# Sigmoid attention and a clipped MLP in one kernel: a third batch multiplied in native float32 beside the first MoE product, with ScalarE's order written out

## The chip, the cores and the metric

The kernel runs on one core of one Trainium2 chip. The metric is the device time of one execution in microseconds. A core has a matrix engine (TensorE, PE), a vector engine (VectorE, DVE), an activation engine (ScalarE, ACT), a general engine (GpSimd, POOL) and a queue that only issues transfers (SyncE, SP). Each takes its instructions in the order in which they stand; they wait for each other through semaphores.

## What is computed

Eight batches of twelve heads, 448 tokens, head size 64. Attention uses a sigmoid in place of a softmax, and its output goes through an MLP with a clipped gate (called MoE here). All inputs are float32 except that the two weight matrices come as float64 (the reference's weights are never cast down).

```
scores = scale * np.matmul(q, k.transpose(0, 1, 3, 2)) - np.log(S)
attn = 1.0 / (1.0 + np.exp(-scores))
x = np.matmul(attn, v)          # then (B, H, S, D) -> (B*S, H*D) = 3584 x 768
h = x @ w_in                    # 768 x 2048
g = h * np.clip(h + 3.0, 0.0, 6.0) / 6.0
out = g @ w_out                 # 2048 x 768
```

## The kernel before

**Units.** Two heads form a pair `p`; a batch has 6 pairs, so there are 48. A pair has `NST` = 4 steps: three over 128 keys of both heads, one over the last 64 keys. Step `s` is step `s % 4` of pair `s // 4`; `scores(s)` issues the products of k and q and the sigmoid of their sum, `av(s)` the products of v and the sigmoid. The tokens of all batches are also cut into seven blocks of 512; `moe_in(t)` yields the 288 products of block `t` with w_in, 18 for each of 16 columns `fc`, evacuates each column's PSUM tile `ph` (two buffers) through ACT and DVE into `g`, and stores `g` in DRAM (`gd`). A last stage multiplies `g` by w_out; the change doesn't touch it.

**Two kinds of product.** In the first `NB` = 2 batches (pairs below `PA` = 12) PE multiplies float32 as it is ("native"): one product for each head, on half of PE's rows or columns, two heads side by side; the profile counts two instructions for each. From the third batch on, every operand is split into a high and a low part (`qh`, `ql`, `ka`, `ah`, `al`), and three or four faster products take the place of one. The split costs work elsewhere: `prep` and `prep_block` cast and subtract on DVE, POOL and ACT, each sigmoid is computed twice (`ah`, `a`, L209 and L210), and DVE subtracts them (`al`, L211).

**w_in.** It comes as float64 and is decoded in 32 chunks of 128x384 by `split_f64`: a transfer, then on ACT an absolute value (L51, "Abs" below), five DVE steps (L52 to L58), a sum on POOL (L61), a cast on ACT (L62) that is the high part, and a subtraction on POOL (L63) that is the low part. Column `fc` needs chunks 2`fc` and 2`fc`+1. A chunk stands in borrowed buffers: the pair `qh`/`ql`, or `pend`.

**Order.** PE's order is the order of the code. All other engines are ordered by a scheduler with a timeline of its own. The code runs the 48 native steps in rounds of two (`scores(s)`, `scores(s+1)`, `av(s-2)`, `av(s-1)`), and asks for 24 chunks in them; then it issues 72 products of block 0 (`EX`) with the other 8 chunks; then the third batch's 24 split steps, with 216 products of block 0 spread among them, nine a step. In fact the scheduler has all 32 chunks decoded by the end of the native steps. From step 72 on, each batch's 24 steps carry the 288 products of one block. At step 73 `flush` turns the columns of the last batch that belong to the next block (`pend`) into high and low parts: six casts and six subtractions.

Of the kernel before, what the change touches and what calls it, by code (L numbers as in the profile page):

```python
# [9 lines left out]
F32 = mybir.dt.float32  # L10
# [8 lines left out]
P = 128  # L19
# [19 lines left out]
NWE = 8
NEA = 5  # L40
# [3 lines left out]
halves = (slice(0, D), slice(D, P))  # L44


def split_f64(nc, hi, lo, st, a, b):

    low, high = st[:, :, 0], st[:, :, 1]
    ai, bi = a.bitcast(I32), b.bitcast(I32)  # L50
    nc.scalar.activation(a, high.bitcast(F32), AF.Abs, bias=0.0, scale=2.0**-112)  # L51
    nc.vector.tensor_scalar_min(a, a, F64_TOP)  # L52
    nc.vector.tensor_scalar(out=ai, in0=ai, scalar1=3, scalar2=None, op0=ALU.logical_shift_left)
    nc.vector.scalar_tensor_tensor(  # L54
        out=ai, in0=high, scalar=-(2**31), in1=ai, op0=ALU.bitwise_and, op1=ALU.bitwise_or
    )
    nc.vector.tensor_scalar(out=bi, in0=ai, scalar1=-(2**23), scalar2=None, op0=ALU.bitwise_and)  # L57
    nc.vector.scalar_tensor_tensor(  # L58
        out=b, in0=low.bitcast(U32), scalar=2.0**-52, in1=b, op0=ALU.mult, op1=ALU.mult
    )  # L60
    nc.gpsimd.tensor_tensor(out=a, in0=a, in1=b, op=ALU.add)  # L61
    nc.scalar.copy(hi, a)  # L62
    nc.gpsimd.tensor_tensor(out=lo, in0=a, in1=hi.bitcast(F32), op=ALU.subtract)  # L63
# [13 lines left out]
def tile_kernel(ctx: ExitStack, tc: tile.TileContext, qk, vP, wi, wo, outT):  # L77
# [39 lines left out]
    def load_native(p):  # L117
        b, hp = divmod(p, NP)
        t = att.tile([P, 2, S], F32, tag="ka", name=f"qkn_{p}")
        v = att.tile([P, 2 * NC, D], F32, tag=("vv", "vv", "vr")[p % 3], name=f"vn_{p}", bufs=(2, 2, 1)[p % 3])  # L120
        nc.sync.dma_start(out=t, in_=qk[b, hp])
        for j in range(2):
            nc.sync.dma_start(out=kbn[p % 3][halves[j], halves[j]], in_=qk[b, hp, halves[j], 1, NC * P :])
        nc.sync.dma_start(out=v, in_=vP[b, hp, :, : 2 * NC])
        for j in range(2):
            nc.sync.dma_start(out=vbn[p % 3][halves[j], halves[j]], in_=vP[b, hp, halves[j], 2 * NC])
        ops[p] = t[:, 0], t[:, 1], v
# [88 lines left out]
    def block(t, cc):  # L216
# [3 lines left out]
            xb[t, cc] = x[:, 0], x[:, 1]  # L220
        return xb[t, cc]

    def flush(b):

        t, c0, _, n = pieces(b)[1]
        for cc in range(NCC):
            xh, xl = (x[:, c0 : c0 + n] for x in block(t, cc))
            x = pend[b][:, cc, :n]
            nc.vector.tensor_copy(xh, x)
            nc.vector.tensor_tensor(out=xl, in0=x, in1=xh.bitcast(F32), op=ALU.subtract)  # L230

    def av(s):
        p, c = divmod(s, NST)
        b, hp = divmod(p, NP)
        last = c == NC
        if p < PA:
            if c == 0:
                pv[p] = ps_a.tile([P, 512], F32, tag=f"pv{p % 2}", name=f"pv_{p}")
            _, a = at.pop(s)
            pt, v = pv[p], ops[p][2]  # L240
            for j in range(2):
                v_, a_ = (vbn[p % 3][:, halves[j]], a[:, 0]) if last else (v[:, j * NC + c], a[:, j])
                nc.tensor.matmul(pt[halves[j], :S], v_, a_, start=(c == 0), stop=last)
            if last:
                for t, c0, q0, n in pieces(b):
                    xh, xl = (x[:, c0 : c0 + n] for x in block(t, hp))
                    nc.scalar.copy(xh, pt[:, q0 : q0 + n])
                    nc.vector.tensor_tensor(out=xl, in0=pt[:, q0 : q0 + n], in1=xh.bitcast(F32), op=ALU.subtract)
            return
        vv = ops[p][3]  # L250
        if c == 0:
            pv[p] = [ps_a.tile([P, 512], F32, tag=f"pv{u}", name=f"pv{u}_{p}") for u in range(2)]
        sc, ah, al = at.pop(s)
        if last:
            vbh, vbl = blk[p % 2]["vbh"], blk[p % 2]["vbl"]
# [8 lines left out]
            nc.gpsimd.tensor_tensor(out=xl, in0=x[:, :n], in1=xh.bitcast(F32), op=ALU.subtract)
            for _, _, q0, n in rest:
                if b not in pend:
                    pend[b] = xpl.tile([P, NCC, PEND], F32, tag="pend", name=f"pend_{b}")
                nc.vector.tensor_tensor(out=pend[b][:, hp, :n], in0=out[:, q0 : q0 + n], in1=x[:, q0 : q0 + n], op=ALU.add)
            return
        for a_ in (ah, al):  # L270
            for j in range(2):
                nc.tensor.matmul(  # L272
                    pv[p][j][:, :S], vv[:, j, c, :], a_[:, j],
                    start=(c == 0 and a_ is ah), stop=(c == NC - 1 and a_ is al),
                )
        if c == NC - 1:
# [8 lines left out]
    evac = []  # L285

    def load_wi(n):
        fc, u = divmod(n, 2)
        hc = NCC // 2
        w = hc * P  # L290
        if u == 0:
            wt = win[fc // GF].tile([P, 2, NCC, P], F32R, tag=f"wi{fc}", name=f"wi_{fc}")
            wih[fc], wil[fc] = wt[:, 0], wt[:, 1]
        cs = slice(u * hc, (u + 1) * hc)
        hi, lo = (w_[fc][:, cs].rearrange("p c f -> p (c f)") for w_ in (wih, wil))
        if n % 3 == 2:
# [27 lines left out]
    nwi = 0
    load_native(0)
    load_native(1)
    for s in range(0, SB, 2):
        p, c = divmod(s, NST)
        scores(s)
        scores(s + 1)  # L330
        for u in (s - 2, s - 1):
            if u >= 0:
                av(u)
        if c == 2 and p + 2 < PA:
            load_native(p + 2)
        if p == PA - 2 and c == 0:
            load(PA)
        while nwi < NWA and nwi * SB < (s + 2) * NWA:
            load_wi(nwi)
            nwi += 1  # L340
        if s == 0:
            for u in range(2):
                for t in blk[u].values():
                    for j in range(2):
                        nc.gpsimd.tensor_copy(t[halves[j], halves[1 - j]], vbn[0][halves[j], halves[1 - j]])
    av(SB - 2)
    av(SB - 1)

    moe = moe_in(0)
    for n in range(EX):  # L350
        while nwi < 2 * NFC and (nwi - NWA) * NBW <= n:
            load_wi(nwi)
            nwi += 1
        next(moe)
# [5 lines left out]
    for s in range(SB, NSTEP + 1):  # L360
        p, c = divmod(s, NST)
        b = p // NP
        if s < NSTEP:
# [4 lines left out]
                prep(p + 1)  # L368
            if c == 3 and p + 2 < B * NP:
                load(p + 2)  # L370
        if s % BS == 1 and s > SB + BS:
            for _ in moe:
                pass
            flush(b - 1)
            moe = moe_in(b - 2)
        if s > SB:
            quota += KM if s > SB + BS else KM - EX / BS
        for _ in range(KB if c == 0 else KM):
            if quota >= 1:
                next(moe, None)  # L380
# [16 lines left out]
    def load_wo(ec, pool):  # L397
# [4 lines left out]
        for u in range(NFC * P // WPC):  # L402
# [105 lines left out]
```

## Time and profile before

| | |
|---|---|
| median of 3 runs | 1306.04 us (1305.58 to 1306.68) |
| profiled execution | 1307.34 us, of which the span is 1305.5 |
| PE busy in the span | 1251.2 us (96%) |
| DVE busy | 814.4 us (62%) |
| ACT busy | 556.9 us (43%) |
| POOL busy | 370.2 us (28%) |
| transfers | 145.87 MB, mean 112 GB/s |
| native stage | 0 to 143 us |

The share of busy time is a mean over stages with different limits; a stage has to be read by itself, by who waits there for whom. A row of the timeline gives the start and the length in us, the engine, the line, what is written from what, and in brackets the idle time before it and what ended it. In a row by groups the columns behind the bar are busy us in all, mean ns of one, and idle time before with its releasers. A row of the waits gives us in total, how often, and the longest.

### The profile page before, as it was taken

The page shows a single profiled execution, that of the slowest core. Times are in us where ns is not written, and L with a number is a line of the kernel's source. Part 1 is how long each engine was busy: PE and PEld are TensorE (multiplying, and loading weights), DVE is VectorE, ACT ScalarE, POOL GpSimd, SP SyncE. Part 2 cuts the span into 40 slices and gives each one's busy share as a digit, 9 for nine tenths or more (in the row PEclk, how much of TensorE's full clock was granted, in tenths as well). Part 3 has the DMA queues.
Part 4 walks back from the last instruction along what each step waited for, and adds up shares of the span by engine and source line. Part 5 has one row for each costly group of instructions (what it writes and reads, how often), then busy time and mean ns, then how long its engine had stood idle before and what let it go on. Part 6 is the DMA issues. An engine that isn't in the chain of part 4 may idle for free.

```text
span 1305.5 us, 15392 instructions
## 1 busy us (share of the span) xinstructions
PE 1251.2 (96%) x5496; PEld 990.4 (76%) x5496; DVE 814.4 (62%) x1362; ACT 556.9 (43%) x716; POOL 370.2 (28%) x392
## 2 busy tenths in 40 slices
PE   6776999999999999999999999999999999999998
PEld 1222588788888888888888887787888888888887
DVE  5977589988988888888898658968130303030300
ACT  4565367665666656665666644424020202020200
POOL 4565334333333333333333224554000000000000
PEclk9789999999999999999999999999999999999999
DMA  7554433343334333334333137743322222222000
GB/s 212 166 154 137 120 106 103 103 119 103 111 105 119 106 100 100 112 111 111 111 112 104 48 114 242 265 146 128 113 85 93 85 92 86 92 85 93 25 25 25
DMA packets 67566, 145.87 MB, mean 112 GB/s; under 512 B 10912, under 2 KB 35488, under 8 KB 63904
## 3 DMA queue, kind: packets, MB, share of 16 engines
q1 hardware_dynamic: 67488, 144.87, 35.5%
q8 instruction: 44, 0.72, 0.2%
q14 instruction: 34, 0.28, 0.1%
HBM read 104.46 MB, written 40.37 MB: 111 GB/s over the span
## 4 chain that ended last, share of the span: by engine, by line
PE 74%; DVE 13%; DMA 5%; issue 3%; ACT 2%; POOL 2%; SPq 1%; POOLq 0%; ACTq 0%; DVEq 0%
PE po L461 30%; PE ph L312 28%; PE pv L272 6%; PE sc L204 3%; PE sc L205 3%; DMA ws<-wo 2%; PE sc L258 2%; DMA wis<-wi 1%; PE sc L201 1%; DVE wa L54 1%; DMA wiqh<-wi 1%; DVE wb L58 1%; DVE wb L57 1%; DVE ql L152 1%; DVE g L317 1%
## 5 line engine op out<-in xcount | busy, mean ns | idle before, releaser
L312 PE MATMUL ph<-x,wi 128*128 128x512 f32 x2016 | 497.9, 394 | 4.8 <-DVE g L317 3.8
L312 PEld LDWEIGHTS ph<-x,wi 128*128 128x128 f32 x2016 | 377.9, 188 | 86.3 <-DVE g L317 6.3
L461 PE MATMUL po<-gh,wol 128*128 128x512 f32 x672 | 262.4, 390 | 1.0 <-POOL wol L63 1.0
L461 PE MATMUL po<-gh,woh 128*128 128x512 f32 x672 | 262.2, 390 | 1.2 <-ACT woh L62 1.2
L461 PE MATMUL po<-gl,woh 128*128 128x512 f32 x672 | 262.0, 390 | 0.0
L468 DVE TENSOR_SCALAR o<-po 128x512 f32<-128x512 f32 x42 | 29.0, 690 | 292.7 <-PE po L461 292.7
L211 DVE TENSOR_TENSOR al<-a,ah 128x896 fp32r<-128x896 f32 (+1 forms) x144 | 170.0, 1181 | 56.7 <-ACT a L210 55.7
L421 ACT CAST gh<-gr 128x2048 fp32r<-128x2048 f32 x28 | 53.4, 1912 | 288.3 <-PE po L461 288.2
L209 ACT ACTIVATE ah<-sc,bias_s 128x896 fp32r<-128x896 f32 (+1 forms) x144 | 131.8, 915 | 80.2 <-PE sc L201 38.7
L148 POOL TENSOR_TENSOR ka<-qkr,ka 64x448 fp32r<-64x448 f32 x72 | 111.7, 1552 | 146.7 <-issue 126.7
L461 PEld LDWEIGHTS po<-gh,wol 128*128 128x128 f32 x672 | 126.5, 188 | 28.1 <-POOL wol L63 1.8
L461 PEld LDWEIGHTS po<-gh,woh 128*128 128x128 f32 x672 | 126.6, 188 | 27.9 <-ACT woh L62 1.6
L461 PEld LDWEIGHTS po<-gl,woh 128*128 128x128 f32 x672 | 126.6, 188 | 26.2
L210 ACT ACTIVATE a<-sc,bias_s 128x896 f32<-128x896 f32 (+1 forms) x144 | 131.1, 911 | 9.5 <-DVE al L211 8.5
L316 ACT ACTIVATE g<-ph,bias 128x512 f32<-128x512 f32 x112 | 77.2, 689 | 63.6 <-PE ph L312 58.8
L158 POOL TENSOR_TENSOR vv<-vr,vv 128x192 fp32r<-128x192 f32 x72 | 42.6, 611 | 171.9 <-issue 168.1
L317 DVE SCALAR_TENSOR_TENSOR g<-g,ph 128x512 f32<-128x512 f32 x112 | 76.2, 680 | 16.7 <-ACT g L316 16.2
L422 DVE TENSOR_TENSOR gl<-gr,gh 128x2048 fp32r<-128x2048 f32 x28 | 63.9, 2288 | 27.4 <-ACT gh L421 27.4
L204 PE MATMUL sc<-qh,ka 128*128 128x448 f32 x216 | 79.2, 367 | 0.1
L205 PE MATMUL sc<-ql,ka 128*128 128x448 f32 x216 | 79.1, 366 | 0.0
L152 DVE TENSOR_TENSOR ql<-qkr,qh 128x896 fp32r<-128x896 f32 x36 | 68.9, 1913 | 4.7 <-ACT qh L151 0.9
L192 PE MATMUL sc<-qkn 64*128 64x448 f32 x144 | 41.6, 681 | 25.2 <-ACT a L194 21.1
(84 smaller groups left out, 1354.6 us busy)
## 6 DMA issues: line engine op xcount, KB each, us to landing
qkr<-qk SPq DMA_DIRECT2D x144, 224.0 KB, 4.1
gd<-g SPq DMA_DIRECT2D x112, 256.0 KB, 2.6
gr<-gd SPq DMA_DIRECT2D x28, 1024.0 KB, 5.6
ws<-wo SPq DMA_DIRECT2D x24, 512.0 KB, 4.5
outT<-o SPq DMA_DIRECT2D x42, 256.0 KB, 2.0
wiqh<-wi SPq DMA_DIRECT2D x22, 384.0 KB, 3.4
vr<-vP SPq DMA_DIRECT2D x36, 224.0 KB, 2.5
qkn<-qk SPq DMA_DIRECT2D x12, 448.0 KB, 4.1
```

The lines of the kernel that those rows point to most:

```text
L148: nc.gpsimd.tensor_tensor(out=ka[other, j], in0=kr[other, j], in1=ka.bitcast(F32)[other, j], op=ALU.subtract)
L152: nc.vector.tensor_tensor(out=ql, in0=qr, in1=qh.bitcast(F32), op=ALU.subtract)
L204: nc.tensor.matmul(sc[:, j, :S], ka[:, j, cs], qh[:, j], start=True, stop=False)
L205: nc.tensor.matmul(sc[:, j, :S], ka[:, j, cs], ql[:, j], start=False, stop=True)
L209: nc.scalar.activation(ah[:, js], sc[:, js, :S], AF.Sigmoid, bias=bias_s, scale=scale)
L210: nc.scalar.activation(a[:, js], sc[:, js, :S], AF.Sigmoid, bias=bias_s, scale=scale)
L211: nc.vector.tensor_tensor(out=al[:, js], in0=a[:, js], in1=ah.bitcast(F32)[:, js], op=ALU.subtract)
L272: nc.tensor.matmul(pv[p][j][:, :S], vv[:, j, c, :], a_[:, j], start=(c == 0 and a_ is ah), stop=(c == NC - 1 and a_ is al),)
L312: nc.tensor.matmul(ph, w[:, cc], x, start=(n == 0), stop=(n == 3 * NCC - 1))
L316: i1 = nc.scalar.activation(g, ph, AF.Relu, bias=bias_3, scale=1.0)
L317: i2 = nc.vector.scalar_tensor_tensor(out=g, in0=g, scalar=6.0, in1=ph, op0=ALU.min, op1=ALU.mult)
L461: nc.tensor.matmul(po[t, ec], w[:, fc], x[:, u], start=(fc == 0 and n == 0), stop=(fc == NFC - 1 and n == 2))
```

## The change

`NB` = 3: the third batch is native too, so there are 72 native steps and 18 native pairs. The first 48 run as before, with 17 chunks (`NWA`) asked for instead of 24. In the other 24, twelve rounds, each round has 23 products of block 0 (`K2`) behind its two native steps: 276 of the 288. The other 12 come behind step 72's scores; the 72 products in a block of their own are gone. The remaining 15 chunks are asked for in these rounds, 1.5 a round.

`split_f64` is cut in two. `load_wi` is a generator with stages: the transfer; then, two rounds later (one round later from chunk 17 on), `join_f64` with Abs, the DVE steps and POOL's sum; then, one round later, `split_f32` with ACT's cast and POOL's subtraction. `feed` takes every chunk on its way one stage further in each round. A fourth place to stand in is added: chunks may also use the buffer `qkr`, the raw q and k of a split pair. The third of the native v tiles goes to the buffer of `qp0` instead of `vr`, so that pair 18's v can be loaded early. A native batch's columns for the block after next go into `pend` by a copy and are split by `flush`.

ACT's order, like PE's, is the order of the code in all 72 native steps. Outside them, and on DVE, POOL and SP, the scheduler decides as before.

```diff
-PA = 2 * NP
+NB = 3
+PA = NB * NP
+P0 = (NB - 1) * NP
-EX = 72
-NWA = 24
-NBW = 9
+K2 = 23
+NWA = 17
+NWG = 1.5
+NSL = 4
...
-def split_f64(nc, hi, lo, st, a, b):
+def join_f64(nc, st, a, b):
...
     nc.gpsimd.tensor_tensor(out=a, in0=a, in1=b, op=ALU.add)
+
+def split_f32(nc, hi, lo, a):
     nc.scalar.copy(hi, a)
     nc.gpsimd.tensor_tensor(out=lo, in0=a, in1=hi.bitcast(F32), op=ALU.subtract)
...
-                for t, c0, q0, n in pieces(b):
+                for u, (t, c0, q0, n) in enumerate(pieces(b)):
+                    if u and b == NB - 1:
+                        hold(b)
+                        nc.vector.tensor_copy(pend[b][:, hp, :n], pt[:, q0 : q0 + n])
+                        continue
...
-        if n % 3 == 2:
+        own = n % NSL if n < NWA else n % (NSL - 1)
+        if own == 2:
+            sa = att.tile([P, 4 * w], I32, tag="qkr", name=f"wis_{n}", bufs=1)
+            st, ab = sa[:, : 2 * w], sa[:, 2 * w :]
+        elif own == 3:
...
         nc.sync.dma_start(out=st, in_=wi[fc, :, u * w : (u + 1) * w])
-        split_f64(nc, hi, lo, st, ab[:, :w], ab[:, w:])
+        yield
+        if n < NWA:
+            yield
+        join_f64(nc, st, ab[:, :w], ab[:, w:])
+        yield
+        split_f32(nc, hi, lo, ab[:, :w])
...
+    with tc.manual_schedule(engines={mybir.EngineType.PE, mybir.EngineType.Activation}):
+        load_native(0)
+        feed(1)
+        load_native(1)
+        for s in range(0, SB, 2):
...
+            if s < P0 * NST:
+                feed((s + 2) * NWA // (P0 * NST) + 1)
+            else:
+                feed(NWA + int((s + 2 - P0 * NST) / 2 * NWG) + 1)
+                if p == PA - 2 and c == 2:
+                    load(PA)
+                moe = moe or moe_in(0)
+                for _ in range(K2):
+                    next(moe)
...
-        if s > SB:
-            quota += KM if s > SB + BS else KM - EX / BS
+        quota += KM
```

**ACT in the first steps.** A name ends in its number: `a_2` is the sigmoid of step 2, `wiql_0` chunk 0's working buffer, `wi_0` column 0's weights. Before, the scheduler put the decode steps between the sigmoids of one round:

```order
L194 ACTIVATE a_0_162<-sc_0_159,bias_s_115 128x896
L194 ACTIVATE a_1_167<-sc_1_164,bias_s_115 128x896
L51 ACTIVATE wiql_0_171<-wiqh_0_170 128x384
L194 ACTIVATE a_2_201<-sc_2_198,bias_s_115 128x896
L51 ACTIVATE wiql_1_222<-wiqh_1_221 128x384
L194 ACTIVATE a_3_206<-sc_3_203,bias_s_115 128x448
L62 CAST wi_0_169<-wiql_0_171 128x384
L51 ACTIVATE wis_2_251<-wis_2_251 128x384
L51 ACTIVATE wiql_3_286<-wiqh_3_285 128x384
L194 ACTIVATE a_4_236<-sc_4_233,bias_s_115 128x896
L62 CAST wi_0_169<-wiql_1_222 128x384
```

Now the two sigmoids of a round come first, then the cast of v's product where a pair ends, then the decode: the cast of the chunk before, and Abs of the next one. From step 6 to step 11:

```order
L201 ACTIVATE a_6_247<-sc_6_244,bias_s_115 128x896
L201 ACTIVATE a_7_252<-sc_7_249,bias_s_115 128x448
L54 ACTIVATE wiql_1_220<-wiqh_1_219 128x384
L201 ACTIVATE a_8_277<-sc_8_274,bias_s_115 128x896
L201 ACTIVATE a_9_282<-sc_9_279,bias_s_115 128x896
L262 CAST x_0_1_288<-pv_1_254 128x448
L69 CAST wi_0_151<-wiql_1_220 128x384
L54 ACTIVATE wis_2_242<-wis_2_242 128x384
L201 ACTIVATE a_10_305<-sc_10_302,bias_s_115 128x896
L201 ACTIVATE a_11_310<-sc_11_307,bias_s_115 128x448
L69 CAST wi_1_241<-wis_2_242 128x384
```

Chunks 1 and 2 here are a run: Abs of 1 in one round, its cast and Abs of 2 in the next, cast of 2 in the third. Up to step 47 the runs are chunk 0, then 1-2, 3-4, 5-7, 8-9, 10-12, 13-14, then 15.

**DVE in the first steps.** The decode of chunk 0 has five steps in a row before; `wis` and `wiql` are working buffers:

```order
L52 TENSOR_SCALAR wiql_0_171<-wiql_0_171 128x384
L53 TENSOR_SCALAR wiql_0_171<-wiql_0_171 128x384
L54 SCALAR_TENSOR_TENSOR wiql_0_171<-wiqh_0_170,wiql_0_171 128x384
L57 TENSOR_SCALAR wiql_0_171<-wiql_0_171 128x384
L58 SCALAR_TENSOR_TENSOR wiql_0_171<-wiqh_0_170,wiql_0_171 128x384
L52 TENSOR_SCALAR wiql_1_222<-wiql_1_222 128x384
```

Now a cast that belongs to `prep` of pair 18 stands among them; its input `vr_18` is the sixteenth entry of SP's queue:

```order
L55 TENSOR_SCALAR wiql_0_153<-wiql_0_153 128x384
L56 TENSOR_SCALAR wiql_0_153<-wiql_0_153 128x384
L57 SCALAR_TENSOR_TENSOR wiql_0_153<-wiqh_0_152,wiql_0_153 128x384
L168 CAST vbh_0_135<-vr_18_1493 64x64 x2
L60 TENSOR_SCALAR wiql_0_153<-wiql_0_153 128x384
L61 SCALAR_TENSOR_TENSOR wiql_0_153<-wiqh_0_152,wiql_0_153 128x384
L263 TENSOR_TENSOR x_0_0_236<-pv_0_199,x_0_0_236 128x448
```

**DVE behind the third batch.** Before, the flush (L229, L230, from `pend_2`) stands among the split steps 71 and 72; `ka_19` and `ql_19` were made a pair earlier:

```order
L229 CAST x_2_1_2094<-pend_2_1313 128x320
L229 CAST x_2_2_2097<-pend_2_1313 128x320
L157 CAST vv_19_2147<-vr_19_2010 128x3x64 x2
L230 TENSOR_TENSOR x_2_0_2091<-pend_2_1313,x_2_0_2091 128x320
L282 TENSOR_TENSOR x_17_2034<-pv0_17_1952,x_17_2034 64x448
L282 TENSOR_TENSOR x_17_2034<-pv1_17_1953,x_17_2034 64x448
L230 TENSOR_TENSOR x_2_1_2094<-pend_2_1313,x_2_1_2094 128x320
L230 TENSOR_TENSOR x_2_2_2097<-pend_2_1313,x_2_2_2097 128x320
L229 CAST x_2_3_2100<-pend_2_1313 128x320
L161 CAST vbh_1_139<-vr_19_2010 64x64 x2
L229 CAST x_2_4_2103<-pend_2_1313 128x320
L211 TENSOR_TENSOR al_72_2045<-a_72_2046,ah_72_2044 128x896
```

Now nine of the flush's twelve steps (L240, L241), with `g` and the last native product's columns (L259, L263), stand ahead of step 72's `al`. The first cast of the flush is two rows above these, and right above it pair 19's `ql`:

```order
L241 TENSOR_TENSOR x_2_0_1713<-pend_2_1006,x_2_0_1713 128x320
L240 CAST x_2_1_1716<-pend_2_1006 128x320
L182 CAST qp0_18_1699<-qh_18_1641 64x448 x2
L241 TENSOR_TENSOR x_2_1_1716<-pend_2_1006,x_2_1_1716 128x320
L263 TENSOR_TENSOR x_1_5_870<-pv_17_1596,x_1_5_870 128x128
L259 COPY pend_2_1006<-pv_17_1596 128x320
L240 CAST x_2_2_1719<-pend_2_1006 128x320
L241 TENSOR_TENSOR x_2_2_1719<-pend_2_1006,x_2_2_1719 128x320
L240 CAST x_2_3_1722<-pend_2_1006 128x320
L241 TENSOR_TENSOR x_2_3_1722<-pend_2_1006,x_2_3_1722 128x320
L240 CAST x_2_4_1725<-pend_2_1006 128x320
L218 TENSOR_TENSOR al_72_1671<-a_72_1672,ah_72_1670 128x896
```

`qh_19`, on which `ql_19` waits, is cast on ACT behind the cast of chunk 31; its q and k are loaded into `qkr`, one buffer, which `ql_18` has to leave first. On POOL the low part of chunk 31 stands behind the two subtractions that make `ka_19`.

More of the change, by code (lines that the diff above doesn't have):

```diff
@@ L119, in load_native @@
         t = att.tile([P, 2, S], F32, tag="ka", name=f"qkn_{p}")
-        v = att.tile([P, 2 * NC, D], F32, tag=("vv", "vv", "vr")[p % 3], name=f"vn_{p}", bufs=(2, 2, 1)[p % 3])
+        v = att.tile([P, 2 * NC, D], F32, tag=("vv", "vv", "qp0")[p % 3], name=f"vn_{p}", bufs=(2, 2, 1)[p % 3])
         nc.sync.dma_start(out=t, in_=qk[b, hp])
@@ L221, in block, with hold @@
         return xb[t, cc]
+    def hold(b):
+        if b not in pend:
+            pend[b] = xpl.tile([P, NCC, PEND], F32, tag="pend", name=f"pend_{b}")
     def flush(b):
@@ L265, in av @@
             for _, _, q0, n in rest:
-                if b not in pend:
-                    pend[b] = xpl.tile([P, NCC, PEND], F32, tag="pend", name=f"pend_{b}")
+                hold(b)
                 nc.vector.tensor_tensor(out=pend[b][:, hp, :n], in0=out[:, q0 : q0 + n], in1=x[:, q0 : q0 + n], op=ALU.add)
@@ L319, in moe_in @@
             nc.sync.dma_start(out=gd[t][fc // GF][:, fc % GF], in_=g)
-    ctx.enter_context(tc.manual_schedule(engines={mybir.EngineType.PE}))
[L324 to L354, printed above, removed]
+    nwi = 0
+    way = []
+    def feed(upto):
+        nonlocal nwi
+        for x in way[:]:
+            if next(x, way) is way:
+                way.remove(x)
+        while nwi < min(upto, 2 * NFC):
+            x = load_wi(nwi)
+            next(x)
+            way.append(x)
+            nwi += 1
@@ new lines, in tile_kernel @@
+    moe = None
+    with tc.manual_schedule(engines={mybir.EngineType.PE, mybir.EngineType.Activation}):
[3 more added lines that the diff above has]
+        for s in range(0, SB, 2):
+            p, c = divmod(s, NST)
+            scores(s)
+            scores(s + 1)
+            for u in (s - 2, s - 1):
+                if u >= 0:
+                    av(u)
+            if c == 2 and p + 2 < PA:
+                load_native(p + 2)
+            if s < P0 * NST:
[7 more added lines that the diff above has]
+                    next(moe)
+            if s == 0:
+                for u in range(2):
+                    for t in blk[u].values():
+                        for j in range(2):
+                            nc.gpsimd.tensor_copy(t[halves[j], halves[1 - j]], vbn[0][halves[j], halves[1 - j]])
+        av(SB - 2)
+        av(SB - 1)
@@ L370, in tile_kernel @@
                 load(p + 2)
-        if s % BS == 1 and s > SB + BS:
+        if s % BS == 1:
             for _ in moe:
@@ L407, in load_wo @@
             nc.sync.dma_start(out=st, in_=wo[ec, :, us])
-            split_f64(nc, hf[:, us], lf[:, us], st, a, b)
+            join_f64(nc, st, a, b)
+            split_f32(nc, hf[:, us], lf[:, us], a)
             yield
```

## The prediction

> **What bounds the kernel now.** I read the page first: the span, the slices, and the clock row under them.
>
> ```profile
> span 1305.5 us, 15392 instructions
> PE   6776999999999999999999999999999999999998
> DVE  5977589988988888888898658968130303030300
> PEclk9789999999999999999999999999999999999999
> ```
>
> TensorE (PE) is full from the fifth slice on. Only the first four, some 130 us, run at six to seven tenths, and there the granted clock is lowered too. So the change can win time only in that stretch, and the next view cuts it by stage: native steps, the 72 products put behind them, the third batch, its end. The columns are busy us of each engine, then clock, DMA share and GB/s.
>
> ```profile
> 0.00:143.00 143.00, 100.69 (x385) 30.88 (x385) 105.72 (x185) 79.63 (x131) 76.73 (x94) 0.88 0.54 163
> 143.00:161.00 18.00, 18.00 (x80) 14.63 (x79) 9.84 (x21) 3.81 (x7) 5.85 (x11) 1.00 0.45 126
> 161.00:247.00 86.00, 85.18 (x381) 70.72 (x380) 76.78 (x135) 60.37 (x77) 33.90 (x37) 1.00 0.37 104
> 247.00:262.00 15.00, 13.53 (x60) 10.60 (x59) 14.73 (x34) 9.23 (x11) 5.89 (x7) 1.00 0.35 96
> ```
>
> In the native stage no engine is full: PE is busy 101 of 143 us, VectorE (DVE) 106. From 143 us on PE is the bound. The table of waits in the native stage says who waits for whom.
>
> ```profile
> PE sc L192 <- ACT a L194: 21.1, 16, 3.1
> PE sc L190 <- ACT a L194: 16.1, 11, 3.7
> ACT wiql L51 <- DMA wiqh<-wi: 16.7, 9, 2.7
> ACT wi L62 <- POOL wis L61: 11.4, 8, 3.4
> ACT wi L62 <- POOL wiql L61: 11.4, 11, 1.9
> ACT wis L51 <- DMA wis<-wi: 9.3, 7, 3.5
> ```
>
> PE waits 37.2 us for sigmoids. ScalarE (ACT) is late with them because it stands itself in front of decode steps: 26.0 us for w_in that has not landed, 22.8 us for GpSimd's (POOL) sum. A sigmoid behind such a step in ACT's queue waits with it.
>
> What PE needs for two native steps (two score groups, two of attention times v) shows where it flows:
>
> ```profile
> 63.91 1.77 PE L192 MATMUL sc<-qkn 64*128 64x448 f32 x8
> 65.61 0.97 PE L243 MATMUL pv<-a,vn 128*64 128x448 f32 x4
> 66.42 0.92 PE L243 MATMUL pv<-a,vbn 128*64 128x448 f32 x4
> 67.27 1.02 PE L192 MATMUL sc<-qkn 64*128 64x448 f32 x4
> ```
>
> From 63.91 to 67.27 is 3.36 us for two steps. The stage has 24 such rounds: 80.6 us of the 143.
>
> **Native or split, the third batch costs PE the same.** The split rows:
>
> ```profile
> 142.99 17.07 PE L312 MATMUL ph<-x,wi 128*128 128x512 f32 x72
> 159.90 0.37 PE L204 MATMUL sc<-qh,ka 128*128 128x448 f32 x1
> ...
> 161.34 0.37 PE L205 MATMUL sc<-ql,ka 128*128 128x448 f32 x1
> ```
>
> The eight split products start 1.44/7 = 0.206 us apart; a pair has 30, so 6.2 us. Native it has two rounds, 6.7 us. Six pairs: 3 us more, not less. A MoE product takes 16.91/72 = 0.235 us, and block 0's 288 are needed either way. The gain is therefore no saved PE work; it must come from the native stage getting shorter, since 15 of the 32 decodes leave it and ACT's order is new.
>
> **The new native stage.** PE's floor is 3.36 us a round. ACT's order may be slower: where a decode's first step (Abs) ends one round and its cast the next, ACT reaches the cast and waits out the chain between them, five DVE operations and POOL's sum. I call that chain L, from the end of Abs to the end of the sum. Two cases, one undisturbed, one with several chunks in flight:
>
> ```profile
> 82.69 0.57 ACT L51 ACTIVATE wiql<-wiqh 128x384 f32<-128x384 f32 x1 [0.62 <-POOL wi L63]
> ...
> 85.40 0.55 DVE L58 SCALAR_TENSOR_TENSOR wiql<-wiqh,wiql 128x384 f32<-128x384 uint32 x1
> ...
> 86.10 1.00 POOL L61 TENSOR_TENSOR wiql<-wiql 128x384 f32<-128x384 f32 x1 [2.48 <-DVE wiql L58]
> ```
>
> ```profile
> 71.52 0.56 ACT L51 ACTIVATE wis<-wis 128x384 f32<-128x384 f32 x1 [0.48 <-DMA wis<-wi]
> ...
> 76.53 1.98 POOL L61 TENSOR_TENSOR wis<-wis 128x384 f32<-128x384 f32 x1 [4.12 <-DVE wis L58]
> ```
>
> The first gives L = 87.10 - 83.26 = 3.8 us, the second 78.51 - 72.08 = 6.4. In the new order one chunk is in flight at a time in this stage, so I take a value near the first, 4.0, since POOL's subtraction for the chunk before still runs beside the new one's first DVE steps. Both ends stay for the range.
>
> A DVE step that meets POOL is seen in these two rows, one operation on one shape:
>
> ```profile
> 67.79 1.03 DVE L57 TENSOR_SCALAR wiql<-wiql 128x384 int32<-128x384 int32 x1
> ...
> 77.31 0.35 DVE L57 TENSOR_SCALAR wiql<-wiql 128x384 int32<-128x384 int32 x1
> ```
>
> The Trainium skill (SBUF — State Buffer, Who interferes with whom) states that DVE in its two-port mode and POOL take a shared port pair as a lock for a whole instruction, so the loser blocks. The two rows agree. The rule speaks against this order, which puts the next Abs right behind a cast, where POOL starts its 1.0 us subtraction: by it each such chunk would have about 0.5 us more in L than an undisturbed one, an estimate, and the sum below would be 7 us later than with none.
>
> ACT's other durations are in one view by shape:
>
> ```profile
> L194 ACT ACTIVATE a<-sc,bias_s 128x896 f32<-128x896 f32 x36 | 36.0, 1001 | 4.9 <-PE sc L192 4.9
> L51 ACT ACTIVATE wiql<-wiqh 128x384 f32<-128x384 f32 x22 | 12.3, 557 | 20.1 <-DMA wiqh<-wi 16.7 <-POOL wi L63 1.9 <-DVE wis L54 1.1
> L62 ACT CAST wi<-wiql 128x384 fp32r<-128x384 f32 x22 | 11.2, 509 | 11.5 <-POOL wiql L61 11.4
> ```
>
> A run of m chunks in consecutive rounds then takes ACT two sigmoids (2.0) and m times (Abs 0.56 + L + cast 0.5), that is 2.0 + m (L + 1.06). The new ACT order has, from step 6 on, four runs of two chunks and two of three: 12.0 + 14 (L + 1.06). With L = 4.0 that is 82.8 us; PE's floor for the same 20 rounds is 67.2, so ACT's chain sets this stage.
>
> It begins late. Chunk 0's decode now has a cast of v for pair 18 in its middle on DVE, which waits for the sixteenth entry of SyncE's queue. Ahead of and in that DMA lie 3.4 MB; at the rate of the first 20 us
>
> ```profile
> 0.00:20.00 20.00, 12.28 (x40) 3.94 (x40) 6.61 (x14) 7.64 (x12) 8.11 (x31) 0.91 0.73 219
> ```
>
> of 219 GB/s they take 16 us. Behind it come two DVE steps, two small POOL steps and the sum, about 4 us in all, then chunk 0's cast with the sigmoids of steps 6 and 7 queued behind it: ACT goes on at about 20.5 us. The runs end at 103.3; one sigmoid later step 48 may start, at **104 us** (before: 143.0 for the end of the native stage).
>
> **The new third batch.** Twelve rounds of 23 MoE products and two native steps: 23 x 0.235 + 3.36 = 8.77 us, 105 us in all. What PE has to cover:
>
> ```profile
> L316 ACT ACTIVATE g<-ph,bias 128x512 f32<-128x512 f32 x112 | 77.2, 689 | 63.6 <-PE ph L312 58.8
> ```
>
> A round holds two sigmoids (2.0), 1.25 decodes (1.06 each) and 1.3 evacuations (0.69 each): 4.2 us of ACT in 8.8. A decode took DVE at most 105.7/32 = 3.3 us in the native stage, so with the evacuations some 5 of 8.8. Each lag is a whole round, longer than L. I cost the decodes and the evacuations here at nothing; this rests on the last w_in half arriving, see below. Then two attention groups (1.65 us) and the scores of step 72: 104 + 105 + 1.7 = 211. With its four products (0.8) and block 0's last 12 (2.8), step 73's scores start at 214.6. Before:
>
> ```profile
> 246.93 0.37 PE L204 MATMUL sc<-qh,ka 128*128 128x448 f32 x1
> ...
> 251.10 0.36 PE L204 MATMUL sc<-qh,ka 128*128 128x448 f32 x1
> ...
> 258.77 2.11 PE L312 MATMUL ph<-x,wi 128*128 128x512 f32 x8 [0.99 <-POOL x L264]
> ```
>
> That is 36.5 us earlier than 251.10.
>
> **The seam behind it.** Now the first split pairs are prepared here, beside the flush of the pending columns. On DVE `ql` of pair 18, the casts and `ql` of pair 19 and nine of the flush's 12 steps stand before step 72's `al`. A step of the flush costs some 0.4 us, `ql` 2.0:
>
> ```profile
> L230 DVE TENSOR_TENSOR x<-pend,x 128x320 fp32r<-128x320 f32 x6 | 2.7, 484 | 0.0
> L229 DVE CAST x<-pend 128x320 fp32r<-128x320 f32 x6 | 1.9, 324 | 0.1
> L152 DVE TENSOR_TENSOR ql<-qkr,qh 128x896 fp32r<-128x896 f32 x1 | 2.0, 2037 | 0.0
> ```
>
> Pair 19's load waits for pair 18's `ql`, so I put its `ql` at about 2 us after the scores of step 72; the flush, g and other casts then bring `al` some 3.5 us late, and a ph buffer 0.5. Before lost 1.8 us here (0.99 in the row above and small gaps). Net +2.2, bounds 0 and +8: POOL's subtraction for the last w_in half is queued behind pair 19's `ka`, and PE waits in block 0's last column if that slips. Everything from step 74 on is the same work, bound by PE.
>
> The profiled execution took 1307.3 us (span 1305.5 and 1.8 around it), 1.3 above the median shown. 1307.3 - 36.5 + 2.2 = 1273.0; on the median's footing **1271.7 us**.
>
> **Rivals.**
> - *The chain binds less.* If L is near 3, PE's floor sets the stage: step 48 at about 20.5 + 1.0 + 67.2 = 89 us, 15 us sooner, 1256 to 1263. Against it: 3.8 in the cleanest row. Chance 0.12.
> - *The chain stays as crowded as now.* L of 4.8 to 6.3 costs 14 us for each 1 us: 1283 to 1303. For it: the second row above, and POOL and DVE keep meeting. Against: half as many chunks. Chance 0.17.
> - *Slower than before.* The same queue of ACT, past a point: with L above 6.5 the hand-written order, in which no sigmoid can pass a waiting cast, ends later than the scheduler's order of before: 14 x 2.5 = 35 us are given back; at L = 7, 1314. For it: the 6.4 row lies close. Against: it had three chunks in flight. Chance 0.04.
> - *The clock.* Native groups after idle time run at half pace:
>
> ```profile
> 33.07 1.86 PE L192 MATMUL sc<-qkn 64*128 64x448 f32 x4 [3.12 <-ACT a L194]
> ```
>
>   1.86 against 1.02 for the four of 67.27. If native work held the third batch at the 0.88 of the native stage, its 105 us would be 119: 1286. Against: 1.00 in every window with MoE products. Chance 0.03. The Trainium skill (TensorE: Matmul & The Clock Gate, What's actually happening) says that the clock halves after an idle window and is full again after a busy one; by that rule the third batch runs at 1.00, as the forecast has it.
> - *No gain:* the lead is lost at the seam and in later waits. The stretch from 161 us on is PE-bound with little slack lost, so only the seam could; 1300 to 1306. Chance 0.02.
>
> **How the numbers follow.** The forecast, L between 3.5 and 4.7 with the seam anywhere in its bounds, is 1263 to 1283, chance 0.62. The range reaches down to 1258, half of the first rival, and up to 1290, about half of the second and most of the clock's: 0.62 + 0.07 + 0.08 + 0.03 = 0.8. A measurement tells 0.2%, 2.6 us, from no change. Faster: 0.94; within it 0.02, from the end of the second rival and the last; slower 0.04.
>
> **What would show it.** Right: step 48 near 104 us; in the native stage ACT's casts wait for POOL, its Abs no longer for DMA; a round of the third batch takes 8.8 us at clock 1.00 with PE full; 2 to 4 us of PE waiting for `al` behind the scores of step 72. Wrong: rounds of 3.4 us throughout (chain too dear in my sum), PE waiting on `a` for over 15 us by the old waits, MoE products waiting for `wi` or ph, or a first round of the third batch that starts after 115 us.

## The result, and the profile after

| | before | after |
|---|---|---|
| median, us | 1305.81 (1304.91 to 1306.68, 4 runs) | **1268.43** (1267.84 to 1269.65, 4 runs) |
| ratio to before | 1 | **0.9715**, 95% interval 0.9698 to 0.9732 |
| profiled execution, us | 1307.3 | 1268.95 (span 1267.1) |
| step 48's scores, us | 159.90 | 102.84 |
| step 73's scores, us | 251.10 | 215.53 |

The forecast was 1271.7 us, so it was 3.3 us too high. The page of the changed kernel, its span and slices:

```profile
span 1267.1 us, 15222 instructions
...
PE   7889999999999999999999999999999999999998
...
DVE  2455557888878888887988589866030303030300
...
PEclk8999999999999999999999999999999999999999
```

The part where PE is not full has shrunk from four slices to three, and DVE, which was at five to nine tenths in the first four, is now at two to five. The stages of the changed kernel, cut at step 48 and at step 72 (columns as in the prediction's table of stages):

```profile
0.00:102.80 102.80, 83.78 (x376) 27.87 (x376) 43.40 (x93) 60.91 (x96) 35.24 (x60) 0.97 0.56 167
102.80:211.80 109.00, 108.96 (x476) 64.84 (x476) 64.29 (x132) 49.94 (x83) 43.20 (x45) 1.00 0.47 135
211.80:262.00 50.20, 50.20 (x231) 42.97 (x230) 43.77 (x83) 31.29 (x40) 14.79 (x16) 1.00 0.40 115
```

From 102.8 us on PE has no gap worth naming. DVE carries 15 decodes in the third batch and still is busy only 64 of 109 us. What is left to lose lies in the first row, 19 us of PE. The waits there, up to 105 us:

```profile
ACT wi L69 <- POOL wiql L64: 15.5, 7, 5.8
PE sc L199 <- ACT a L201: 14.6, 12, 4.5
...
ACT wi L69 <- POOL wis L64: 11.9, 7, 2.5
```

PE waits for sigmoids, and ACT waits 27.4 us in front of casts for POOL's sum. ACT no longer waits for w_in to land: those two rows, 26 us together before, have gone.

**Where the 38.4 us of span come from**, on the rows of both traces:

- The native part ends 38.5 us earlier: 142.99 before; 102.84 after, plus 1.65 for two groups of attention times v that now stand behind step 48's scores.
- The third batch costs PE 3.3 us more: from there to step 73's scores it is 111.0 us now, and was 107.8 without its one wait of 0.36.
- Two microseconds of before have gone at the seam: the wait of 0.36, and 1.66 from step 73's scores to step 75's (10.42 us before, with one wait of 0.99 in them; 8.76 now).
- The other 1.2 us lie spread over a thousand microseconds of the same work.

### The profile page after: what moved, and what is told of

Read it like the earlier page. It is cut to its first block, busy times and chain, and to the rows that moved or that the text cites. A ratio compares the mean times of both kernels' runs of the same rounds, so it can differ in the third digit from the quotient of the medians.

```text
span 1267.1 us, 15222 instructions
## 1 busy us (share of the span) xinstructions
PE 1238.2 (98%) x5508; PEld 965.9 (76%) x5508; DVE 728.7 (58%) x1236; ACT 523.2 (41%) x680; POOL 327.3 (26%) x350
## 4 chain that ended last, share of the span: by engine, by line
PE 83%; DVE 7%; DMA 3%; issue 2%; ACT 2%; POOL 2%; SPq 1%; POOLq 0%; ACTq 0%; DVEq 0%
PE ph L336 32%; PE po L500 31%; PE pv L286 6%; PE sc L211 3%; PE sc L212 3%; PE pv L254 2%; PE sc L199 2%; DMA ws<-wo 2%; PE sc L208 1%; PE sc L273 1%; DVE wa L57 1%; DVE wb L60 1%; DVE wb L61 1%; ACT a L201 1%; POOL wa L64 1%
## 5 line engine op out<-in xcount | busy, mean ns | idle before, releaser
L218 DVE TENSOR_TENSOR al<-a,ah 128x896 fp32r<-128x896 f32 x120 | 142.8, 1190 | 50.2 <-ACT a L217 49.4
L216 ACT ACTIVATE ah<-sc,bias_s 128x896 fp32r<-128x896 f32 x120 | 110.0, 917 | 76.2 <-PE sc L212 39.3
L155 POOL TENSOR_TENSOR ka<-qkr,ka 64x448 fp32r<-64x448 f32 x60 | 91.2, 1521 | 129.1 <-issue 110.9
L217 ACT ACTIVATE a<-sc,bias_s 128x896 f32<-128x896 f32 x120 | 109.3, 911 | 1.7 <-DVE al L218 0.7
L461 DVE TENSOR_TENSOR gl<-gr,gh 128x2048 fp32r<-128x2048 f32 x28 | 63.9, 2288 | 27.4 <-ACT gh L460 27.4
L201 ACT ACTIVATE a<-sc,bias_s 128x896 f32<-128x896 f32 x72 | 62.2, 910 | 30.2 <-PE sc L199 30.0
L165 POOL TENSOR_TENSOR vv<-vr,vv 128x192 fp32r<-128x192 f32 x60 | 34.8, 600 | 146.2 <-issue 136.5
L199 PE MATMUL sc<-qkn 64*128 64x448 f32 x216 | 53.1, 600 | 18.7 <-ACT a L201 14.6
L211 PE MATMUL sc<-qh,ka 128*128 128x448 f32 x180 | 66.0, 367 | 0.0
L212 PE MATMUL sc<-ql,ka 128*128 128x448 f32 x180 | 65.9, 366 | 0.0
(85 smaller groups left out, 1252.7 us busy)
```

Of the source, the lines that this page charges most:

```text
L155: nc.gpsimd.tensor_tensor(out=ka[other, j], in0=kr[other, j], in1=ka.bitcast(F32)[other, j], op=ALU.subtract)
L199: nc.tensor.matmul(sc[:, j, :S], k[halves[j], cs], q[halves[j]], start=True, stop=True)
L211: nc.tensor.matmul(sc[:, j, :S], ka[:, j, cs], qh[:, j], start=True, stop=False)
L212: nc.tensor.matmul(sc[:, j, :S], ka[:, j, cs], ql[:, j], start=False, stop=True)
L216: nc.scalar.activation(ah[:, js], sc[:, js, :S], AF.Sigmoid, bias=bias_s, scale=scale)
L217: nc.scalar.activation(a[:, js], sc[:, js, :S], AF.Sigmoid, bias=bias_s, scale=scale)
```

## The experiments

The theory under test (A): the native stage ends when ACT's queue lets it. A cast that waits out the chain L holds up the sigmoids behind it, and everything from step 48 on is PE-bound and only moves along. Nine kernels were tried, each of them timed in several rounds beside the kernel before.

| run | ratio to before, 95% interval | us | first MoE product, us |
|---|---|---|---|
| the kernel before | 1 | 1305.81 | 142.99 |
| the change | 0.9715 (0.9698 to 0.9732) | 1268.43 | 106.20 |
| e1_scheduler_order | 1.0055 (1.0036 to 1.0074) | 1313.34 | 149.71 |
| e2_no_lag | 1.0215 (1.0193 to 1.0237) | 1334.37 | 142.78 |
| e3_chunks24 | 0.9841 (0.9825 to 0.9857) | 1285.29 | 123.34 |
| e4_cast_later | 0.9591 (0.9575 to 0.9607) | 1252.72 | 90.06 |
| e5_v18_later | 0.9672 (0.9660 to 0.9685) | 1263.08 | 100.41 |
| e6_abs_first | 0.9659 (0.9646 to 0.9671) | 1261.93 | 99.22 |
| e7_abs_first_v18 | 0.9624 (0.9610 to 0.9637) | 1256.90 | 93.45 |
| e8_cast_later_v18 | 0.9591 (0.9578 to 0.9604) | 1252.08 | 89.65 |
| e9_two_batches | 1.0048 (1.0034 to 1.0063) | 1312.79 | 121.33 |

In five of them (e3 to e7) time and first product move together: against the changed kernel the first product moves by +17.1, -16.1, -5.8, -7.0 and -12.8 us, the time by +16.9, -15.7, -5.4, -6.5 and -11.5. That is the second half of theory A: behind step 48 little is lost or won, at most 1.3 us.

### ACT's order left to the scheduler

```diff
-    with tc.manual_schedule(engines={mybir.EngineType.PE, mybir.EngineType.Activation}):
+    with tc.manual_schedule(engines={mybir.EngineType.PE}):
```

> The changed kernel with ACT's order in the native steps left to the scheduler again; chunks, lags and the native third batch stay. Theory A (the native stage ends when ACT's queue lets it: sigmoids stand behind decode steps that wait) says that Abs and casts come back in front of sigmoids and PE's waits for sigmoids grow from the 19 us of the changed kernel towards half of the 37 us per 32 chunks of the kernel before plus the clock lost with them: 1272 to 1285 us. Theory B (the gain comes from the native third batch and from fewer decodes, whatever ACT's order) says 1266 to 1271, as the changed kernel's 1268.

1313.34 us: all of the gain is gone, and 7.5 us more. Both theories had it too low. The waits of this kernel, up to 146 us, and ACT's casts of chunks in the same time, by shape:

```profile
PE sc L199 <- ACT a L201: 39.7, 21, 5.3
ACT wi L69 <- POOL wiql L64: 21.9, 13, 4.6
ACT wis L54 <- DMA wis<-wi: 13.3, 6, 3.2
```

```profile
L69 ACT CAST wi<-wiql 128x384 fp32r<-128x384 f32 x19 | 9.7, 510 | 22.0 <-POOL wiql L64 21.9
L69 ACT CAST wi<-wis 128x384 fp32r<-128x384 f32 x13 | 6.6, 511 | 11.2 <-POOL wis L64 11.1
```

PE waits as long for sigmoids as it did in the kernel before (37.2 us). And 19 + 13 are all 32 chunks: the code asks for 17 in the first two batches, but the scheduler, free on ACT too, has pulled the other 15 forward, as it did before. So the run doesn't keep the chunks where they were, as its expectation says; it takes back the move of 15 decodes with the order. ACT's queue, at one place:

```profile
64.70 0.61 ACT L201 ACTIVATE a<-sc,bias_s 128x448 f32<-128x448 f32 x1
65.21 0.50 ACT L69 CAST wi<-wiql 128x384 fp32r<-128x384 f32 x1
68.50 0.51 ACT L69 CAST wi<-wiql 128x384 fp32r<-128x384 f32 x1 [2.79 <-POOL wiql L64]
68.92 1.00 ACT L201 ACTIVATE a<-sc,bias_s 128x896 f32<-128x896 f32 x1
```

Two casts, one of them with 2.8 us of waiting, stand between the two sigmoids that PE needs next. PE's longest single wait for a sigmoid, 5.3 us ahead of step 48's scores, is of another kind: ACT's cast of pair 18's `qh`, which the scheduler put among the native sigmoids, waits 5.1 us for its transfer. So the written-out order, with the place that it gives to the decodes, is worth 45 us of this change, and the native third batch without it gives none. What the order of the sigmoids alone is worth with 17 decodes in the stage is not shown by this run.

### No round between POOL's sum and the cast

```diff
         join_f64(nc, st, ab[:, :w], ab[:, w:])
-        yield
         split_f32(nc, hi, lo, ab[:, :w])
```

> The changed kernel with the last stage of a decode taken back: cast and subtraction stand in the same round as Abs, so ACT waits out the whole chain L of 3.5 to 3.9 us (read from the changed kernel's trace) with no sigmoid between. Theory A: a round with a chunk costs ACT 2.0 + 0.56 + 3.7 + 0.5 = 6.8 us, 16 such rounds and 4 without from 21 us on put step 48 at about 142 in place of 102.8 us: 1300 to 1315 in all. Theory B: the decodes are the same work, up to 1275.

1334.37 us. The native stage grew by 36.6 us, the time by 65.9: the third batch was hit too, which the expectation had left out. The queue of PE in this kernel's third batch:

```profile
148.35 1.02 PE L199 MATMUL sc<-qkn 64*128 64x448 f32 x4
...
151.71 3.30 PE L335 MATMUL ph<-x,wi 128*128 128x512 f32 x13
156.87 2.60 PE L335 MATMUL ph<-x,wi 128*128 128x512 f32 x10 [1.87 <-DVE g L340]
159.40 1.77 PE L199 MATMUL sc<-qkn 64*128 64x448 f32 x8
```

This round takes 11.05 us, from 148.35 to 159.40, where the changed kernel's take 8.93: the evacuations of `ph` and the sigmoids stand behind casts that wait. A lag of one round pays in both stages.

### 24 chunks in the native stage instead of 17

```diff
-NWA = 17
+NWA = 24
```

> The changed kernel with 24 in place of 17 chunks decoded in the first 48 steps, one a round, so that every round has a cast that waits for the Abs of the round before. Theory A: one run of chunks with 0.56 + L + 0.5 = 4.9 us each, from 20.7 us on 23 x 4.9 + 2.0, so step 48 near 136 in place of 102.8 us: 1298 to 1306. Theory B: seven more decodes are some 17 us of DVE beside idle, 1268 to 1275.

1285.29 us, below A's numbers. Step 48 starts at 119.99, against 102.84. The price that A takes for a round was right, the number of rounds was not: the expectation counted 23 rounds, but only the 20 behind step 6 hold a waiting cast. ACT's rows of the cast of chunk 0 and of the twentieth behind it:

```profile
20.23 0.51 ACT L69 CAST wi<-wiql 128x384 fp32r<-128x384 f32 x1 [5.03 <-POOL wiql L64]
...
118.08 0.51 ACT L69 CAST wi<-wiql 128x384 fp32r<-128x384 f32 x1 [1.06 <-POOL wiql L64]
```

That is 4.89 us a round, where the formula's 0.56 + 3.9 + 0.5 is 4.96; the rest of the cast and one sigmoid later step 48 begins. Seven decodes fewer in the third batch made nothing shorter there: the cover of that stage has room to spare.

### The casts a further round later

```diff
         join_f64(nc, st, ab[:, :w], ab[:, w:])
         yield
+        if n < NWA:
+            yield
         split_f32(nc, hi, lo, ab[:, :w])
```

> The changed kernel with the cast of each of the first 17 chunks one round later still, so that nothing on ACT has to wait out L. Theory A: from 23 us on the rounds run at PE's 3.36 us, step 48 near 88 in place of 102.8 us: 1252 to 1258. Theory B: no change, 1266 to 1270, or slower where the buffers that a chunk holds for a round longer make its transfer late.

1252.72 us, as A had it, and better than both kernels. PE's slices on this kernel's page, its native stage cut by time up to step 48's scores, and ACT's only wait for POOL up to 90 us:

```profile
PE   8999999999999999999999998999999999999998
```

```profile
0.00:20.00 20.00, 14.65 (x59) 5.15 (x61) 2.94 (x8) 9.59 (x12) 5.68 (x31) 1.00 0.63 200
20.00:40.00 20.00, 20.00 (x98) 6.79 (x96) 13.32 (x25) 15.94 (x25) 9.67 (x10) 1.00 0.67 197
...
60.00:86.70 26.70, 26.70 (x129) 8.82 (x129) 17.01 (x34) 20.55 (x35) 12.61 (x12) 1.00 0.60 184
```

```profile
ACT wi L69 <- POOL wiql L64: 3.3, 1, 3.3
```

The 27.4 us in which ACT stood before casts have shrunk to 3.3, all of it at one cast, and from 20 us on PE does the same work without a gap. That is the stage's floor: 24 rounds of 3.36 us are 80.6, and step 48 starts at 86.7 with 5.4 us lost in the first 20. Nearly all of these are PE's waits for q and k to land:

```profile
PE sc L199 <- DMA qkn<-qk: 5.3, 2, 4.0
```

The decodes are the same and only the waits went, so the waits were the bound.

### Pair 18's v loaded later

```diff
-        v = att.tile([P, 2 * NC, D], F32, tag=("vv", "vv", "qp0")[p % 3], name=f"vn_{p}", bufs=(2, 2, 1)[p % 3])
+        v = att.tile([P, 2 * NC, D], F32, tag=("vv", "vv", "vr" if p < P0 else "qp0")[p % 3], name=f"vn_{p}", bufs=(2, 2, 1)[p % 3])
```

> The changed kernel with the native v tiles of pairs 2, 5, 8 and 11 in the buffer that pair 18's v goes to, so that this load and its cast on DVE can't stand in the middle of chunk 0's decode. If that cast sets the start (chunk 0's cast on ACT at 20.7 us, PE idle for 4.5 us and at half clock for some 3 us after it), step 48 comes 3.5 to 7 us earlier: 1261 to 1265. If the load of pair 2's q and k, issued right behind, sets the start instead, under 2 us: 1266 to 1269.

1263.08 us. With `vr` in use, the early load of `vr_18` can't happen, and its cast leaves chunk 0's decode. ACT's cast of chunk 0 in this kernel:

```profile
14.99 0.51 ACT L69 CAST wi<-wiql 128x384 fp32r<-128x384 f32 x1
```

In the changed kernel it stands at 20.72, after a wait of 5.81. The whole stage moved by 5.8.

### Abs of the next chunk ahead of the cast

```diff
-        for x in way[:]:
+        for x in way[::-1]:
```

> The changed kernel with Abs of the next chunk ahead of the cast of the one before, in each round. The work and the lags stay; only Abs no longer waits behind a waiting cast. Theory A: two chains are under way at once, so a run needs (L + 3.1)/2 = 3.4 us a round, PE's floor; step 48 some 9 to 11 us earlier, 1257 to 1261. Theory B: no change, 1266 to 1270. A third case: DVE and POOL now carry two chunks at once and L grows towards the 6.4 us seen in the kernel before, 1262 to 1268.

1261.93 us, 0.9 above A's numbers. The chain of the next chunk starts before ACT waits for the last one, and that won 6.5 us. But L itself grew, as one chunk shows in the rows of this kernel:

```profile
28.51 0.56 ACT L54 ACTIVATE wis<-wis 128x384 f32<-128x384 f32 x1
...
29.54 1.01 POOL L70 TENSOR_TENSOR wi<-wiql,wi 128x384 fp32r<-128x384 f32 x1 [3.39 <-ACT wi L69]
29.57 1.20 DVE L56 TENSOR_SCALAR wis<-wis 128x384 int32<-128x384 int32 x1
...
32.42 0.99 POOL L64 TENSOR_TENSOR wis<-wis 128x384 f32<-128x384 f32 x1 [1.87 <-DVE wis L61]
```

From the end of Abs (29.07) to the end of the sum (33.41) are 4.3 us: POOL's subtraction meets a DVE step that takes 1.20 us here and 0.36 alone.

### Both of these together

The edits of the last two runs in one kernel.

> The two edits of Abs first and of pair 18's v later, together. If both of their reasons hold and they touch different stretches, the gains add: 1250 to 1257.

1256.90 us, 11.5 below the changed kernel; apart they gave 5.4 and 6.5, so they add. The stall at the start and the waiting casts behind it are two separate losses in ACT's queue.

### The later cast and the later v together

> The changed kernel with both edits that were tried apart: each cast of the first 17 chunks one more round behind its sum, and the third native v tile in the buffer vr for the first two batches, so that pair 18's v is loaded late and its cast no longer stands in chunk 0's decode. If both lie on ACT's queue they can only partly add: the first edit puts chunk 0's cast a round later, and what the start lost before (some 6 us) is then partly hidden by it. Chain theory: 1247 to 1251, first MoE product at 84 to 88 us, rounds near PE's floor of 3.36 us. Rival (the late cast alone already hides the start): 1251 to 1254, the same as that edit alone. Rival (PE's floor with the halved clock after gaps is reached): also near 1252, with waits of PE for sigmoids under 5 us and a granted clock near 1.00.

1252.08 us: no better than the later cast alone (the same ratio, 0.9591), as its two rivals had it. ACT's row of chunk 0's cast with the later cast alone, and then with both edits:

```profile
20.81 0.51 ACT L69 CAST wi<-wiql 128x384 fp32r<-128x384 f32 x1 [3.32 <-POOL wiql L64]
```

```profile
17.69 0.50 ACT L69 CAST wi<-wiql 128x384 fp32r<-128x384 f32 x1
```

ACT is there 3.1 us earlier and doesn't wait, yet the first MoE product comes only 0.4 us sooner. PE waits there for no sigmoid up to 96 us, only 4.7 us for q and k to land. With ACT out of the way PE's own work and these first transfers are the bound, and a cause on ACT's queue is worth nothing more.

### ACT's order and the lags without a native third batch

The kernel before, with two native batches: ACT's order by hand in its 24 native rounds, the decode in stages with a round between them, 24 chunks there and the other 8 beside the 72 products.

```diff
         nc.sync.dma_start(out=st, in_=wi[fc, :, u * w : (u + 1) * w])
-        split_f64(nc, hi, lo, st, ab[:, :w], ab[:, w:])
+        yield
+        join_f64(nc, st, ab[:, :w], ab[:, w:])
+        yield
+        split_f32(nc, hi, lo, ab[:, :w])
...
+    with tc.manual_schedule(engines={mybir.EngineType.PE, mybir.EngineType.Activation}):
...
+            feed((s + 2) * NWA // SB + 1)
...
+        if n % NBW == 0:
+            feed(NWA + n // NBW + 2)
```

> The kernel before with ACT's order written out in its native steps and the decode in stages one round apart, 24 chunks there, and nothing else: the third batch stays split, the 72 products stay in their own stretch with the other 8 chunks. Theory A, by the chain: 15 + 23 x 4.9 + 2.0, step 48 near 130 in place of 143 us, so 1290 to 1297: a third of the gain. If the order alone carried the gain: 1265 to 1280. If it is worth nothing without the native third batch: 1303 to 1308.

1312.79 us, half a per cent slower than before, and outside all three ranges that were expected. The native stage did end some 19 us sooner (its last products of v at 123.03 us, with three MoE products ahead of them). The stretch behind it gave it all back:

```profile
150.00:170.00 20.00, 8.45 (x27) 6.68 (x28) 17.54 (x28) 8.81 (x13) 11.16 (x10) 0.67 0.39 100
```

```profile
153.93 0.71 PE L214 MATMUL sc<-qh,ka 128*128 128x448 f32 x1 [8.79 <-POOL wiql L61]
159.03 0.74 PE L215 MATMUL sc<-ql,ka 128*128 128x448 f32 x1 [4.40 <-DVE ql L162]
```

PE is busy 8.5 of 20 us, DVE 17.5: the last decodes, which stand in the buffers of `qh` and `ql`, and the split of pair 12 that needs those buffers, meet in front of the first split steps. In the changed kernel those decodes have a batch of native steps beside them that asks little of DVE. That no arrangement with two native batches would do is not shown; this one doesn't.

## Why the prediction held

**What bounds the stage: shown.** The prediction took ACT's chain as what sets the native stage, 2.0 + m (L + 1.06) for a run of m chunks, and PE's floor below it. Taking the wait away (e4) brought the stage to the floor, lengthening the runs (e3) cost what the formula says for the rounds there are, and the rows give L itself. Two chunks of the changed kernel, all engines in order of time:

```profile
36.24 0.58 ACT L54 ACTIVATE wis<-wis 128x384 f32<-128x384 f32 x1
...
36.93 0.35 DVE L55 TENSOR_SCALAR wis<-wis 128x384 f32<-128x384 f32 x1
...
39.34 0.99 POOL L64 TENSOR_TENSOR wis<-wis 128x384 f32<-128x384 f32 x1 [4.13 <-DVE wis L61]
...
40.36 0.51 ACT L69 CAST wi<-wis 128x384 fp32r<-128x384 f32 x1 [2.12 <-POOL wis L64]
...
40.78 0.56 ACT L54 ACTIVATE wiql<-wiqh 128x384 f32<-128x384 f32 x1
40.95 1.01 POOL L70 TENSOR_TENSOR wi<-wis,wi 128x384 fp32r<-128x384 f32 x1 [0.62 <-ACT wi L69]
...
41.44 0.73 DVE L55 TENSOR_SCALAR wiql<-wiql 128x384 f32<-128x384 f32 x1 [2.19 <-ACT wiql L54]
...
44.23 1.00 POOL L64 TENSOR_TENSOR wiql<-wiql 128x384 f32<-128x384 f32 x1 [2.27 <-DVE wiql L61]
```

The first chunk of a run has L = 40.33 - 36.82 = 3.5, the one behind a cast 45.23 - 41.34 = 3.9; of the 14 chunks of the formula five have 3.5 and nine 3.9, where 4.0 was taken for all. In eight of the nine the difference is the one DVE step that meets POOL's subtraction, 0.73 us against 0.35; the ninth (chunk 8) starts its DVE steps 0.5 us after its Abs, and the cause of that is not known. The Trainium skill (SBUF — State Buffer, Who interferes with whom) has the shared port pair held for a whole instruction while the loser blocks; the estimate made from it was 0.5 us for each of 14 chunks, the trace has 0.4 for eight, some 3 us in place of 7. Of the two rows that the prediction set side by side there, the short one isn't a DVE step without POOL: the sum of 76.53, in the prediction's second case of L, runs beside it until 78.51, and there POOL's step was the long one, 1.98 us in place of 1.0.

**The late start: right, in part by luck.** ACT was to go on at 20.5 us, because of the cast of pair 18's v in chunk 0's decode. In the changed kernel:

```profile
18.16 0.41 DVE L168 CAST vbh<-vr 64x64 fp32r<-64x64 f32 x2 [6.20 <-DMA vr<-vP]
```

```profile
20.72 0.51 ACT L69 CAST wi<-wiql 128x384 fp32r<-128x384 f32 x1 [5.81 <-POOL wiql L64]
```

ACT goes on with the next sigmoid at 21.14. Run e5 took the cast of v away and with it 5.4 us, so the cause is right. But v landed at 18.2 where 16 was estimated, and the steps behind it took 2.5 us to the end of the sum where 4 were: two errors that nearly cancel.

Step 48 came at 102.84, forecast 104: 0.6 later at the start, 2.2 less in the runs (80.6 from 21.14 to the next sigmoid at 101.78, forecast 82.8), 0.4 more behind them. With the L of the rows the formula gives 79.4, which is 3.4 less than forecast. In the first run ACT didn't wait for the chain but for PE: chunk 1's sum ends at 26.54, its cast starts at 28.71, as PE's eight products of 22.20, behind an idle time of 4.53 us, took 3.36 us where those of 31.50 took 1.77. The formula has no such term.

**The third batch: right, with a small term too low.** PE's rows at its end and behind it:

```profile
201.22 1.02 PE L199 MATMUL sc<-qkn 64*128 64x448 f32 x4
...
204.58 5.64 PE L336 MATMUL ph<-x,wi 128*128 128x512 f32 x23
210.15 0.97 PE L254 MATMUL pv<-a,vn 128*64 128x448 f32 x4
...
211.80 0.47 PE L211 MATMUL sc<-qh,ka 128*128 128x448 f32 x1
...
215.53 0.36 PE L211 MATMUL sc<-qh,ka 128*128 128x448 f32 x1
...
219.12 0.57 PE L286 MATMUL pv<-ah,vv 128*128 128x448 f32 x2
```

A round is 8.93 us (201.22 to 210.15) where 8.77 was summed: its native part is 3.36 as taken, its 23 products 5.57, not 23 x 0.235 = 5.41. Twelve rounds make 2 us of it. The clock stayed at 1.00, so the rival on the clock falls, as the rule of the Trainium skill (TensorE: Matmul & The Clock Gate, What's actually happening) cited in the prediction had it; decodes and evacuations did cost nothing. That native or split costs PE the same within 3 us was the prediction's reason to look for the gain elsewhere; measured were 3.3.

**The seam: the size was wrong.** The prediction charged 4 us for a late `al` and a `ph` buffer, net +2.2. The row of 219.12 has no wait in front of it. DVE's rows in the changed kernel:

```profile
210.58 1.09 DVE L159 TENSOR_TENSOR ql<-qkr,qh 128x896 fp32r<-128x896 f32 x1
...
216.62 1.09 DVE L218 TENSOR_TENSOR al<-a,ah 128x896 fp32r<-128x896 f32 x1
```

The order was as told, nine of the flush's steps between the two. But `ql` of pair 19 starts 1.2 us before the scores of step 72, not 2 us behind them, and takes 1.09 us, not the 2.04 of the row that was used: POOL's half of `ka` of the same pair ended at 209.5, before it began. So `al` ends at 217.7, and PE comes to it at 219.5. None of the 2 to 4 us of waiting for `al` that the prediction named as a sign were seen. This term is where the sum was off: step 73 came 35.6 us earlier and not 36.5, but behind it 2.8 us more were won where 2.2 were to be lost. 0.9 and -5.0 are the 4.1 us between 1273.0 and the 1268.95 of the profiled execution.

**The rivals.** A chain that binds less didn't come by itself; e4 made it, and it gave somewhat more than that rival had in it (1252.7 against 1256 to 1263), as step 48 then starts at 86.7 and not 89, and the seam costs nothing. The crowded chain is out: behind chunk 0 no L is above 3.93. Times at or above the kernel before are seen in e1, e2 and e9: in e2 by the mechanism of the third rival, sigmoids behind casts that wait, in e1 by this and by the decodes that came back, in e9 by the stretch behind the native stage.

**What stays open.** The change has two halves, and neither gave anything alone (e1: 1.0055, e9: 1.0048, together 0.9715). But e1 takes away more than one half, as the scheduler also brought 15 decodes back into the native stage: the waits in ACT's queue are shown, but not how much of the 45 us the order costs and how much the decodes. For e9 it is shown where the time went, but not that a better place for the last eight decodes couldn't be found.

## What to carry to other kernels

- In a queue that works in order, count how long each instruction will wait, not how long it runs: of 17 casts of 0.5 us, 14 waited 27.4 us in all here, because they stood in front of sigmoids while their input was still being made. One more round between the two took 24 us of that waiting away and won 16 us.
- When the engine at the bound is full behind a stage, any microsecond won in that stage shows in the total; find that stage's own floor (here 24 rounds of 3.36 us) and compare.
- Moving work that the bottleneck doesn't do (decodes) beside a stretch where the bottleneck is full and their engine is idle can be worth a dearer version of the bottleneck's own work (3.3 us here): the two runs in which the decodes came ahead of the third batch (e1, e9) lost the whole gain, though neither shows that no other arrangement would keep it.

## What was not expected of the hardware

- `ql` on DVE takes 1.08 us or 2.08 us in one kernel, as the view of its tile from 199 to 226 us shows (shortest, median, longest in ns, then when); the long one starts together with POOL's half of `ka` at 221.7, which reads the same input. The price of such a step at one place of a trace is not its price at another.

```profile
L159 DVE TENSOR_TENSOR ql<-qkr,qh x3: 1084/1093/2080, 200.7 to 221.7; 128x896 fp32r<-128x896 f32 x3
```

- Twenty-three products between native groups take 0.17 us more than 23 of the pace of a long series (5.57 against 5.41). What the 0.17 us are was not tried.
